# The total decay of ten late chunks taken from the last row of an exponential and spread over the partitions by two small DMAs

## The chip, the cores and the metric

The kernel runs on one core of one Trainium2 chip. The core has a TensorE for matmuls (PE in the profile, its weight loads PEld), a VectorE (DVE), a ScalarE (ACT), a GpSimd (POOL) and a SyncE (SP), whose instruction stream issues nearly all DMAs here. Each engine works through its own instructions strictly in order; an instruction that waits holds up everything behind it on that engine. SBUF is the on-chip memory with 128 partitions; PSUM is the memory that PE writes to, eight banks of 2 KB per partition. The metric is the device time of one execution in microseconds, the median of several runs.

## The reference, cut to what matters

```python
def _attn_ref(q, k, v, alpha):                 # 4 x 8 heads x 768 steps x 48
    for t in range(S):
        state = alpha[:, :, t, :, None] * state + np.einsum('bhd,bhe->bhde', k[:, :, t], v[:, :, t])
        y[:, :, t] = np.einsum('bhd,bhde->bhe', q[:, :, t], state)

def _moe_ref(x, w_in, w_spatial, b_spatial, w_out):
    h = np.maximum(x @ w_in, 0.0)              # 384 -> 1024
    u, v = h[..., :512], h[..., 512:]
    v_n = (v - mean(v)) / np.sqrt(var(v) + 1e-06)
    v_s = np.einsum('ts,bsd->btd', w_spatial, v_n) + b_spatial[None, :, None]
    return (u * v_s) @ w_out
```

The first half is a linear attention whose state (48 x 48 per head) decays by `alpha`, a factor for each step and each of the 48 rows. Its output, laid out as 4 x 768 x 384, goes through the second half, a gated MLP that also mixes over the 768 steps.

## The kernel before, in words

**Chunks.** Each of the 4 batches is cut into 6 chunks of 128 steps, so chunks have numbers 0 to 23, and chunk 6b is the first of batch b. Inside a chunk the recurrence is done by matmuls: with A the running product of `alpha` in the chunk, q is multiplied by A, k is divided by A, and the state that is handed on is (old state + k'v) times A at the chunk's last step. This last factor, one number for each head and row, is the *total decay*.

**Steps of one late chunk** (`single(i)`, used for chunks 10 to 23; the early ones are done two or four at a time by other functions). I name them as the code does:

- `acs`, `kcs`, `qcs`, `vcs` (L883): four loads of 192 KB from alpha, k, q, v, issued by SP.
- `lns` (ACT, L888): the logarithm of alpha. `cums` (PE): one matmul with a triangle of ones (L898) puts the running sums of the logarithms into a PSUM bank, with steps on the 128 partitions; four more matmuls with one column each (L901) put the *total* of each row into four spare columns of the same bank, this time with (head, row) on the partitions.
- `einvs` (ACT, L908) = exp(-sums) in SBUF, and `eexps` (ACT, L910) = exp(sums), written back over the sums in PSUM.
- `ebc` (ACT, L915): two small exponentials take the totals from the spare columns into the tile `bc`, (head, row) on the partitions. Chunk 11, 17 and 23 are the last of their batch and need no total.
- `kts`, `qts` (L189): k times `einvs` (mostly POOL), q times `eexps` (DVE). `trk` (PE, L988) turns both for a pair of chunks, `evs` (ACT, DVE) copies them out; `upd` (PE, L932) is k'v; `sc`, `ms`, `y`, `xe` make the chunk's output x.
- The carry: `z` (DVE, L393) = k'v + old state; `S` (L189, on DVE for the first chunk of a batch and for chunk 19, else on POOL) = z times `bc`; `sb`, a bf16 copy. `y` of the next chunk and `S` of the next chunk need it.

**The MLP** runs between the chunks, a batch behind: `v`, `u`, `s`, `o` are its matmuls (all recorded at L1005), `ve`, `ue`, `bn`, `rs`, `nm`, `vn`, `se`, `g`, `oe` the steps of DVE, ACT and POOL between them; `vn` is the normalised v, `s` the mixing over steps. `st` (L1184, SP) stores 192 KB of output.

**What sets the order.** A table, `PLAN`, lists every step with its engine and its PSUM banks. The kernel emits the steps in that order, so each engine's queue is fixed in advance, SP's included. A word such as `S549` is step 549 on SP. SP's queue in the stretch that the change touches reads: ... vcs 14, kcs 14, acs 17, qcs 17, kcs 16, vcs 15, qcs 16, kcs 17, vcs 16, then the loads of chunks 18 to 21 in a mixed order (the last of them vcs 20), a store, and the loads of chunks 22 and 23.

Of the kernel before, what the change touches and what calls it, by code (L numbers as in the profile page):

```python
# [15 lines left out]
FP32 = mybir.dt.float32  # L16
# [44 lines left out]
S548 S611 S561 S551 S549 A358 A363 D418 D423 P511@7 P369@3 P413@0 P374@2 P380@1 D414 D417 A261 A512 P378@0 D422 A498  # L61
D364 A375 A564 P263@5 P499@6 G244 G332 G409 G256 A370 A379 A513 D371 G415 A500 A501 P419@0 P424@3 A425 G517 G505 G503
D381 D382 D516 G515 A420 P266@2 P269@4 A502 A365 A383 A270 D366 D504 P429@0 P426@1 P438@3 P440@6 D384 A368 A430 A427
P436@4 A437 A441 A385 D264 D439 P272@0 D367 D267 D428 D431 D386 P521@1 P372@4 A514 A273 P565@6 P376@2 A377 A432 A552
P442@7 A568 P529@0 D443 D522 P456@3 D433 D434 A435 A566 A567 D373 P452@7 P553@1 P518@2,5 A519 A554 A556 D520 A555 P457
D458 D530 D570 G569 G523 G557 G459 P444@4 P445 P448@5 D446 P453 D454 P468@6 P449 D558 D450 P533@7,4 P524@2,0 P572@1,3
D525 G451 G455 P472@5 P469 P460@2 P473 D526 D534 D535 G531 G447 D474 S623 A559 P575@7 D576 A573 P461 S625 S612 S563
A615 D470 D462 P616@4 P527@5 P536@1 A627 S613 A574 P579@7,3 P588@6,0 G577 A617 A528 D589 A618 A537 P628@5 A629 A571
G475 P538@2 A630 P464@1 S624 S614 S730 S718 S721 S626 S720 G620 D621 D581 D580 S733 S732 P476@6 G631 G578 P541@3
P584@7 A539 A619 A542 P465 S784 S719 A477 D632 P634@5,4 D590 A636 D466 D585 S731 A722 P591@3 S786 S772 S785 S773 S835  # L70
S774 A592 S787 S775 G622 G532 P582@1 A583 D635 D540 P637@7 P482@6 A633 A483 P723@5 G586 G471 D638 G639 A724 P645@3,4
P640@0,2 D543 G463 G587 P479@7 P604@6 P596@1 D646 D642 D641 A734 A726 D647 G729 G467 A605 A741 G727 P593@3 P600@6 A594
P735@0 D606 D595 A738 D480 P648@4 P643@3 A544 D545 D546 D597 A649 P488@2 A644 A788 A601 A489 D547 P653@4 P660@7 P745@6
A654 D746 D655 A736 A607 D608 D610 P491@3 P664@4 A661 A665 A737 P650@6 A492 A776 G739 P598@1 D651 D609 P485@4 D652
A486 A725 D747 P666@7 A667 D740 P602@6 P662@4 P789@3 A656 A603 P676@7 P672@0 P753@6 A599 A790 A791 P777@1 A778 A792
A779 S484 S847 S836 S837 A839 A783 S838 S848 A663 S849 D657 D658 D659 D754 D728 P677 P673 P680@6 P688@5 D674 P681
P668@0 D794 D755 D678 D782 G781 G795 D682 P799@7 P669 G793 D800 P689 G675 D690 D670 P742@6,4 P796@7,3 A851 A780 D797
P696@5 A743 A798 G683 G679 P808@0 P697 P852@7 P840@6 A841 A842 A853 A843 A854 D744 P748@3,4 P757@1,2 D698 G801 G671
D749 D809 D758 P692@5 P693 D694 D750 P684@3 P703@0 P685 P700@5 G846 D759 A701 D686 P706@4 D856 D845 D707 A704 P760@5
A761 P751@0 A752 A802 P803@6,7 D805 G844 G855 P812@3,2 P858@4,5 G810 G687 G699 G691 A859 G695 D813 P762@0 S850 P861@7  # L80
P765@3 D814 D804 P712@2 P815@6 A756 A763 P806@0 A860 D862 D764 D857 A816 A807 A766 P864@5,7 P869@4,1 S702 P715@6 D866
D871 D767 D870 D865 P828@7 A829 D830 P824@1 P820@3 P817@7 A821 A768 A818 A825 G863 P872@4 A873 S705 A716 S481 S259
S268 S487 S265 S493 S490 S271 S708 S262 S478 S274 G811 P867@5 D819 P826@3 P822@1 D868 P877@4 D769 D771 A827 S717 A831
A823 A878 A770 A713 D832 P874@3 D833 D834 P890@5 P888@1 P884@4 D879 D875 D876 A880 D881 D882 P916@6 P709@2 A710 P896@3
P886@7 P900@0 A887 A889 A885 A891 P892@2 D883 P897 D898 G899 P893 P901 P908@5 P909 D894 D902 P904@2 P905 G903 P917
P912@0 P913 P920@3 D906 D895 D918 G919 D907 P929@6 P923@2 P921 S711 A930 S931 A924 S925 S714 D914 D910 D911 P926@6
G915 D922 P932@2 A933 D927 S928 S934 P938@3 D939 S940 P935@6 A936 S937 P941@3 D942 S943
"""
# [4 lines left out]
QUADS = (0,3)  # L93
PLAIN = (0, 2)
IDLE = 16

# [35 lines left out]
def kernel(  # L132
# [38 lines left out]
    def sb(name, n, shape, dt=BF16):  # L171
        return [consts.tile(shape, dt, name=f"{name}{x}") for x in range(n)]
# [189 lines left out]
    def half(x):  # L362
        return slice(64 * x, 64 * x + 64)
# [64 lines left out]
    def pair(j):  # L428
# [72 lines left out]
        def ebc(_):  # L501
            src = banks[sl_c[1].bank][:, DM:DM + 2 * HP].rearrange("p (hp c) -> p hp c", c=2)
            for s in range(2):
                nc.scalar.activation(out=bcs[j % 4][half(s), :, :, s], in_=src[half(s)], func=AF.Exp)

# [60 lines left out]
        for i in chunks:  # L566
            carry(i, sl_t[i], ("upd", j, "pair"), bcs[j % 4][:, :, i % 2])

# [301 lines left out]
    def single(i):  # L870
# [25 lines left out]
        def cum(_):  # L896
            cm = flat(sl_c)
            nc.tensor.matmul(out=cm[:, 0:DM], lhsT=le_one, rhs=la[:, :, :, 0:D], start=True, stop=True)  # L898
            if not last:
                for hp in range(HP):  # L900
                    nc.tensor.matmul(  # L901
                        out=cm[:, DM + hp:DM + hp + 1], lhsT=la[:, hp].rearrange("p s d -> p (s d)"), rhs=ones_col,
                        start=True, stop=True)

        op(("cums", i), "PE", cum, [("lns", i), ("one",), ("zeros", 2)], take=[sl_c],
           pe=(0.0, 384, 0, 2) if last else (0.241, 1, 0, 10))
        buf = binv[i % 4].rearrange("p (hp s) d -> p hp s d", s=2)
        op(("einvs", i), "ACT", lambda _: nc.scalar.activation(out=buf, in_=sums(), func=AF.Exp, scale=-1.0),  # L908
           [("cums", i)] + readers("kt", j - 2), use=[sl_c])
        op(("eexps", i), "ACT", lambda _: nc.scalar.activation(out=sums(), in_=sums(), func=AF.Exp), [("einvs", i)], use=[sl_c])  # L910
        bc = bcs[j % 4][:, :, ci]
        if not last:
            def ebc(_):
                for s in range(2):
                    nc.scalar.activation(out=bc[half(s), :, s], in_=banks[sl_c.bank][half(s), DM:DM + HP], func=AF.Exp)  # L915
# [312 lines left out]
    for th in range(2):  # L1228
        made[("bb", th)].deps.append(made[("cum", 1, 1)])
    idle = consts.tile([128, 1], FP32, name="idle")  # L1230
    nc.vector.memset(junk, 0.5)  # L1231
# [33 lines left out]
```

## Time and profile before

| what | value |
|---|---|
| time, median of 3 runs (lowest to highest) | 138.53 us (138.37 to 139.0) |
| span of the profiled execution, first to last instruction | 137.9 us |
| PE busy | 130.1 us, 94% |
| DVE / ACT / POOL busy | 120.2 (87%) / 107.7 (78%) / 86.6 us (63%) |
| granted PE clock | 1.00 throughout |
| the chain that ended last | PE 60%, DMA 19%, POOL 8% |

The profiled execution has no time of its own beside its span; the 0.6 us between its span and the median lie before its first and after its last instruction.

How to read the rows: in a timeline a row gives start and length in us, engine, source line, operation, output tile <- input tiles, form and count; instructions of the same kind are merged to one row with `xN`. What stands in brackets is the idle time before it and what ended it. `SPq` is SP's queue: the length of its row is the time that the issue of the DMA held the queue, waiting included. A group's row ends with busy time and mean length in ns, then the idle time before the group's instructions.

### The profile page before, as it was taken

The numbers are of one execution on the slowest core, as the hardware profiler recorded it, in microseconds if no ns is written. First come the engines' busy times: TensorE is split into PE (matmuls) and PEld (weight loads), VectorE is DVE, ScalarE is ACT, GpSimd is POOL, SyncE is SP. The second block draws the span as 40 slices with busy tenths as digits, with TensorE's granted clock in tenths as the row PEclk, the third lists the DMA queues.
The fourth block names the chain that finished last, engine by engine and source line by source line (L and its number), as shares of the span: only waits on it lengthen the run. The fifth ranks groups of instructions, "written<-read, shape, count | busy, mean of one in ns | idle before, by whom it ended". The sixth has DMA issues, their size and how long they took to land.

```text
span 137.9 us, 5298 instructions
## 1 busy us (share of the span) xinstructions
PE 130.1 (94%) x2108; PEld 79.4 (58%) x2122; DVE 120.2 (87%) x300; ACT 107.7 (78%) x261; POOL 86.6 (63%) x146
## 2 busy tenths in 40 slices
PE   6999998999999999799999999999999999999990
PEld 3365555565566556466657676656576765566560
DVE  6259999989989999899899999997999999974960
ACT  3476998999999799699997989999865796953040
POOL 7355899993499799761079989520799841004550
PEclk9999999999999999999999999999999999999999
DMA  3999999499989788699999898999960597101064
GB/s 88 370 372 381 344 349 361 106 373 382 355 162 281 159 168 165 124 186 188 193 204 201 164 209 156 189 186 216 213 134 5 187 349 270 63 0 57 0 233 172
DMA packets 76521, 28.66 MB, mean 208 GB/s; under 512 B 63056, under 2 KB 74960, under 8 KB 76496
## 3 DMA queue, kind: packets, MB, share of 16 engines
q1 hardware_dynamic: 76464, 28.32, 77.8%
q8 instruction: 16, 0.26, 0.8%
q14 instruction: 9, 0.07, 0.2%
q0 software_dynamic: 32, 0.00, 0.0%
HBM read 23.60 MB, written 4.72 MB: 205 GB/s over the span
## 4 chain that ended last, share of the span: by engine, by line
PE 60%; DMA 19%; POOL 8%; issue 3%; SPq 3%; ACT 3%; DVE 0%; POOLq 0%; ACTq 0%
PE bank L1005 43%; DMA raw_w<-in_moe_w_spatial_dram 6%; DMA kc<-in_k_dram 5%; DMA raw_w<-in_moe_w_out_dram 4%; DMA ac<-in_alpha_dram 4%; PE bank L960 3%; SPq L883 3%; PE bank L944 2%; PE bank L988 2%; PE bank L416 2%; POOL w_row L180 2%; POOL kt L189 2%; PE bank L932 1%; PE bank L898 1%; POOL state L189 1%
## 5 line engine op out<-in xcount | busy, mean ns | idle before, releaser
L1005 PE MATMUL bank<-w_spT,vn 128*128 128x384 bf16 x192 | 35.6, 327 | 0.0
L189 POOL TENSOR_TENSOR gT<-vs,uT 128x384 bf16<-128x384 f32 x28 | 25.7, 933 | 14.1 <-DVE vs L1152 14.1
L189 POOL TENSOR_TENSOR kt<-kc,binv 128x384 bf16<-128x384 f32 x22 | 20.2, 928 | 22.3 <-ACT binv L908 15.2
L1005 PEld LDWEIGHTS <-vn 128*128 128x128 bf16 x192 | 17.5, 98 | 11.2 <-issue 0.3
L1005 PE MATMUL bank<-w_in,xT 128*128 128x512 bf16 x58 | 17.4, 380 | 1.6 <-ACT xT L178 0.7
L1005 PE MATMUL bank<-xT,w_in 128*128 128x384 bf16 x96 | 18.7, 326 | 0.0
L1005 PE MATMUL bank<-w_out_sb,gT 128*128 128x384 bf16 (+1 forms) x100 | 18.4, 320 | 0.0
L1152 DVE TENSOR_TENSOR vs<-bank,bsp_bc 128x384 f32<-128x384 f32 x31 | 16.3, 549 | 2.4 <-PE bank L1005 2.3
L949 DVE TENSOR_TENSOR ptm<-bank,mask 128x512 bf16<-128x512 f32 x28 | 17.9, 682 | 0.5 <-PE bank L944 0.3
L178 ACT COPY kqT<-bank 128x512 bf16<-128x512 bf16 (+1 forms) x20 | 15.0, 793 | 3.1 <-PE bank L988 1.9
L1067 DVE BATCH_NORM_STATS2 stats<-v_sb 128x6 f32<-128x512 bf16 x24 | 16.4, 683 | 0.6 <-ACT v_sb L184 0.5
L184 ACT ACTIVATE v_sb<-bank 128x512 bf16<-128x512 f32 x20 | 11.7, 597 | 2.0 <-PE bank L1005 1.7
L184 ACT ACTIVATE uT<-bank 128x384 bf16<-128x384 f32 x27 | 12.4, 494 | 0.7 <-PE bank L1005 0.6
L1005 PEld LDWEIGHTS <-w_in 128*128 128x128 bf16 x96 | 9.0, 97 | 6.7 <-DVE ptm L949 0.3
L189 DVE TENSOR_TENSOR qt<-qc,bank 128x384 bf16<-128x384 f32 x24 | 12.6, 545 | 0.2 <-DMA qc<-in_q_dram 0.2
L1005 PEld LDWEIGHTS <-gT 128*128 128x128 bf16 x100 | 9.2, 98 | 5.8
L178 ACT CAST xT<-bank 128x384 bf16<-128x384 f32 x23 | 10.4, 482 | 1.1 <-PE bank L416 0.8
L843 DVE TENSOR_TENSOR ptm<-bank,mask 128x512 bf16<-128x512 f32 x16 | 10.3, 683 | 0.2 <-PE bank L836 0.2
L242 PE MATMUL bank<-junk 128*128 128x512 f32 (+3 forms) x14 | 8.8, 763 | 1.0 <-DVE junk L1231 1.0
L1005 PEld LDWEIGHTS <-xT 128*128 128x128 bf16 x72 | 6.2, 97 | 6.2 <-ACT xT L178 1.2
L178 ACT COPY raw_w<-bank 128x384 f32<-128x384 f32 x8 | 3.8, 479 | 7.3 <-PE bank L1005 7.2
L393 DVE TENSOR_TENSOR zs<-bank,state 128x384 f32<-128x384 f32 x16 | 8.8, 548 | 0.5 <-PE bank L932 0.4
(162 smaller groups left out, 264.3 us busy)
## 6 DMA issues: line engine op xcount, KB each, us to landing
ac<-in_alpha_dram SPq DMA_DIRECT2D x14, 192.0 KB, 4.4
kc<-in_k_dram SPq DMA_DIRECT2D x14, 192.0 KB, 4.4
qc<-in_q_dram SPq DMA_DIRECT2D x14, 192.0 KB, 4.4
vc<-in_v_dram SPq DMA_DIRECT2D x14, 192.0 KB, 4.2
raw_w<-in_moe_w_spatial_dram SPq DMA_DIRECT2D x3, 768.0 KB, 7.8
out_dram<-raw_w SPq DMA_DIRECT2D x11, 192.0 KB, 2.1
out_dram<-o_sb SPq DMA_DIRECT2D x9, 192.0 KB, 2.0
ac<-in_alpha_dram SPq DMA_DIRECT2D x2, 768.0 KB, 6.7
```

The source lines that it names most:

```text
L178: nc.scalar.copy(out=out, in_=in_)
L184: nc.scalar.activation(out=out, in_=in_, func=AF.Relu)
L189: ENG[eng].tensor_tensor(out=out, in0=in0, in1=in1, op=ALU.mult)
L242: nc.tensor.matmul(out=banks[n][:, 0:cols].rearrange("p (a b) -> p a b", a=4), lhsT=junk, rhs=junk[:, None, 0:cols // 4].to_broadcast([128 ...
L393: lambda _: nc.vector.tensor_tensor(out=zs[i % 3], in0=tp(), in1=state[(i - 1) % 3], op=ALU.add),
L843: nc.vector.tensor_tensor(out=ptm[n2][:, ci, s], in0=banks[sl.bank].rearrange("p (hp t) -> p hp t", hp=HP), in1=mask[:, 3][:, None, :].to_ ...
L883: nc.sync.dma_start(out=t[x].rearrange("p hp s d -> p (hp s) d"), in_=src[b, :, c * C:c * C + C, :].rearrange("h s d -> s h d"))
L949: nc.vector.tensor_tensor(out=ptm[n2][:, ci, s], in0=banks[sl_p[s].bank].rearrange("p (hp t) -> p hp t", hp=HP), in1=mask[:, 2][:, None, : ...
L960: nc.tensor.matmul(out=place(to, 3 * hp + (0, 1, 1, 2)[x]), lhsT=heads(vb, hp, x), rhs=ptm[n2][:, ci, x // 2, hp, :], start=(turn == 0), s ...
L1005: nc.tensor.matmul(out=ps, lhsT=lhsT, rhs=rhs, start=first and n == 0, stop=last and n == len(pairs) - 1)
L1067: nc.vector.bn_stats(out=stats[tt % 2], in_=v_sb[n2][:, tt, :])
L1152: nc.vector.tensor_tensor(out=vs[d], in0=banks[sl.bank][:, 0:TH], in1=bsp_bc[:, th, :], op=ALU.add)
```

## The change

For the ten chunks of the list `BY_DMA` (12 to 22 without 17) the total decay is no longer computed on its own. `cums` loses its four one-column matmuls, and the two `ebc` exponentials on ACT are gone. Instead `eexps` writes exp(sums) to SBUF in fp32 (into one of three tiles of `o_sb`, which are used in turn, with the elements arranged so that one partition's row is ordered by half, row and head pair). The last of its 128 partitions, step 127, holds the total decay, and two DMAs on SP's queue (one for each half, 48 partitions x 4 fp32 values) spread it over the partitions of `bc`. `qts` reads exp(sums) from this SBUF tile instead of the PSUM bank. The layout of `bc` is turned so that the four values of a partition lie together.

`PLAN` gets ten `ebc` words on SP and loses ten on ACT; `eexps` of chunk 18 moves ahead on ACT, to just behind `einvs` 18. All other words stay in their order on their engines. In SP's queue the new words come to stand as follows: `ebc` 13, 12, 15 and 14 between kcs 14 and acs 17; `ebc` 16 between qcs 16 and kcs 17; `ebc` 18, 19, 21 and 20 between vcs 20 and the store; `ebc` 22 between qcs 23 and vcs 23. Because the three tiles are used in turn, `eexps` of a chunk also waits for `qts` and the two DMAs of the chunk three places earlier in the list.

```diff
-D364 A375 A564 P263@5 P499@6 G244 G332 G409 G256 A370 A379 A513 D371 G415 A500 A501 P419@0 P424@3 A425 G517 G505 G503
+D364 A375 A564 P263@5 P499@6 G244 G332 G409 G256 A370 A379 A513 S514 D371 G415 A500 A501 S502 P419@0 P424@3 A425 G517
...
+BY_DMA = (13, 12, 15, 14, 16, 18, 19, 21, 20, 22)
...
-    bcs = sb("bc", 4, [128, HP, 2, 2], FP32)
+    bcs = sb("bc", 4, [128, 2, 2, HP], FP32)
...
-            if not last:
+            if not last and i not in BY_DMA:
                 for hp in range(HP):
                     nc.tensor.matmul(
                         out=cm[:, DM + hp:DM + hp + 1], lhsT=la[:, hp].rearrange("p s d -> p (s d)"), rhs=ones_col,
                         start=True, stop=True)
...
-        op(("eexps", i), "ACT", lambda _: nc.scalar.activation(out=sums(), in_=sums(), func=AF.Exp), [("einvs", i)], use=[sl_c])
-        bc = bcs[j % 4][:, :, ci]
-        if not last:
+        bc = bcs[j % 4][:, ci].rearrange("p s hp -> p hp s")
+        if i in BY_DMA:
+            before = BY_DMA.index(i) - 3
+            decay = o_sb[1 + (before + 2) % 3].rearrange("p (s d hp) -> p s d hp", hp=HP, s=2)
+            made[("decay", i)] = op(
+                ("eexps", i), "ACT", lambda _: nc.scalar.activation(out=decay.rearrange("p s d hp -> p hp s d"), in_=sums(), func=AF.Exp),
+                [("cums", i)] + ([(x, BY_DMA[before]) for x in ("qts", "ebc")] if before >= 0 else [
...
+            def ebc(_):
+                for s in range(2):
+                    nc.sync.dma_start(
+                        out=bcs[j % 4][64 * s:64 * s + D, ci, s], in_=decay[C - 1:C, s])
+
+            op(("ebc", i), "SP", ebc, [("eexps", i), ("zeros", 0), ("S", i - 8)])
...
-        op(("qts", i), "DVE", lambda e: mul(e, qt[:, :, :, 0:D], t["qc"], sums()),
-           [("eexps", i), ("qcs", i), ("zeros", 1 + n2)] + old_q(j), use=[sl_c])
+        op(("qts", i), "DVE", lambda e: mul(e, qt[:, :, :, 0:D], t["qc"], decay.rearrange("p s d hp -> p hp s d") if i in BY_DMA else sums()),
+           [("eexps", i), ("qcs", i), ("zeros", 1 + n2)] + old_q(j), use=[] if i in BY_DMA else [sl_c])
```

More of the change, by code (lines that the diff above doesn't have):

```diff
@@ L69 @@
[L69 to L87, printed above, removed]
+A615 D470 D462 P616@4 P527@5 P536@1 A627 S613 A574 P579@7,3 P588@6,0 G577 A617 A528 D589 A618 S619 A537 P628@5 A629
@@ L503, in ebc @@
             for s in range(2):
-                nc.scalar.activation(out=bcs[j % 4][half(s), :, :, s], in_=src[half(s)], func=AF.Exp)
+                nc.scalar.activation(out=bcs[j % 4][half(s), :, s].rearrange("p c hp -> p hp c"), in_=src[half(s)], func=AF.Exp)
         op(("ebc", j, "pair"), "ACT", ebc,
@@ L566, in pair @@
         for i in chunks:
-            carry(i, sl_t[i], ("upd", j, "pair"), bcs[j % 4][:, :, i % 2])
+            carry(i, sl_t[i], ("upd", j, "pair"), bcs[j % 4][:, i % 2].rearrange("p s hp -> p hp s"))
         for par in range(2):
@@ L905, in single @@
         op(("cums", i), "PE", cum, [("lns", i), ("one",), ("zeros", 2)], take=[sl_c],
-           pe=(0.0, 384, 0, 2) if last else (0.241, 1, 0, 10))
+           pe=(0.0, 384, 0, 2) if last or i in BY_DMA else (0.241, 1, 0, 10))
         buf = binv[i % 4].rearrange("p (hp s) d -> p hp s d", s=2)
@@ L909, in single @@
            [("cums", i)] + readers("kt", j - 2), use=[sl_c])
-        op(("eexps", i), "ACT", lambda _: nc.scalar.activation(out=sums(), in_=sums(), func=AF.Exp), [("einvs", i)], use=[sl_c])
-        bc = bcs[j % 4][:, :, ci]
-        if not last:
+        bc = bcs[j % 4][:, ci].rearrange("p s hp -> p hp s")
[5 more added lines that the diff above has]
+                [("cums", i)] + ([(x, BY_DMA[before]) for x in ("qts", "ebc")] if before >= 0 else [
+                    x for jj in QUADS for x in [("pm", 2 * jj + y) for y in range(4)] + [("upd", jj, "pair"), ("upd", jj + 1, "pair")]]),
+                use=[sl_c])
+            def ebc(_):
[3 more added lines that the diff above has]
+            op(("ebc", i), "SP", ebc, [("eexps", i), ("zeros", 0), ("S", i - 8)])
+        else:
+            op(("eexps", i), "ACT", lambda _: nc.scalar.activation(out=sums(), in_=sums(), func=AF.Exp),
+               [("einvs", i)], use=[sl_c])
+        if not last and i not in BY_DMA:
             def ebc(_):
@@ L1229 @@
         made[("bb", th)].deps.append(made[("cum", 1, 1)])
+    for n in range(12, 15):
+        made[("oe", n)].deps += [made[x, i] for x in ("qts", "ebc") for i in BY_DMA[(n - 11) % 3::3]]
     idle = consts.tile([128, 1], FP32, name="idle")
```

26 lines of the change are left out of this document (22 added, 4 removed).

## The prediction

> **What bounds the kernel now.** I read the page first: shares, slices, DMA issues.
>
> ```profile
> PE 130.1 (94%) x2108; PEld 79.4 (58%) x2122; DVE 120.2 (87%) x300; ACT 107.7 (78%) x261; POOL 86.6 (63%) x146
> ...
> PE   6999998999999999799999999999999999999990
> ...
> DMA  3999999499989788699999898999960597101064
> ...
> PE 60%; DMA 19%; POOL 8%; issue 3%; SPq 3%; ACT 3%; DVE 0%; POOLq 0%; ACTq 0%
> ...
> kc<-in_k_dram SPq DMA_DIRECT2D x14, 192.0 KB, 4.4
> ...
> out_dram<-o_sb SPq DMA_DIRECT2D x9, 192.0 KB, 2.0
> ```
>
> PE is full from slice 17 on (58 us), so any later PE wait adds to the time. DMA is nearly full as well until slice 29. A late load lands 4.4 us after its issue, a store into an emptier queue after 2.0. Next the windows, for the stretch of the new DMAs.
>
> ```profile
> 66.00:96.00 30.00, 29.83 (x469) 19.26 (x470) 28.62 (x67) 27.50 (x71) 18.38 (x24) 1.00 0.96 191
> ```
>
> The columns are window, length, busy PE, PEld, DVE, ACT, POOL, clock, DMA share, GB/s. PE has 0.17 us free in 30, DVE 1.4, and the DMA share is 0.96: loads that fall behind cannot be caught up. Then SP's timeline, since the change puts twenty DMAs and their waits into that queue.
>
> ```profile
> 65.16 0.73 SPq L883 DMA_DIRECT2D kc<-in_k_dram  x1
> 65.99 1.43 SPq L883 DMA_DIRECT2D ac<-in_alpha_dram  x1
> ...
> 71.19 0.79 SPq L883 DMA_DIRECT2D kc<-in_k_dram  x1
> ...
> 80.96 0.37 SPq L883 DMA_DIRECT2D ac<-in_alpha_dram  x1
> ...
> 90.53 2.14 SPq L883 DMA_DIRECT2D vc<-in_v_dram  x2
> 92.75 0.66 SPq L1184 DMA_DIRECT2D out_dram<-w_row  x1
> 93.46 0.42 SPq L883 DMA_DIRECT2D ac<-in_alpha_dram  x1
> ```
>
> These are, in order: kcs 14, acs 17, kcs 17, acs 21, then vcs 21 with vcs 20, a store, acs 23. SP issues without a break. Its queue runs far behind the written order: vcs 20 leaves only at 92.67.
>
> **The change part by part.** First the consumers of the total decay on DVE, in the chunks that begin a batch, and ACT's steps.
>
> ```profile
> 67.11 0.55 DVE L189 TENSOR_TENSOR state<-bank,bc 128x384 f32<-128x384 f32 x1
> 67.57 0.32 DVE L1084 TENSOR_SCALAR shift<-mvs,rstd 128x1 f32<-128x1 f32 x2
> ...
> 90.33 0.56 DVE L189 TENSOR_TENSOR state<-bank,bc 128x384 f32<-128x384 f32 x1
> ...
> 92.16 0.68 DVE L186 TENSOR_SCALAR v_sb<-bank 128x512 bf16<-128x512 f32 x1
> ```
> ```profile
> 67.99 0.81 ACT L1092 ACTIVATE vn<-v_sb,shift,rstd 128x512 bf16<-128x512 bf16 x1 [0.20 <-DVE shift L1084]
> 68.83 0.49 ACT L908 ACTIVATE binv<-bank 128x384 bf16<-128x384 f32 x1
> 69.22 0.49 ACT L910 ACTIVATE bank<-bank 128x384 f32<-128x384 f32 x1
> ...
> 70.91 0.35 ACT L915 ACTIVATE bc<-bank 64x4 f32<-64x4 f32 x2
> 71.28 0.47 ACT L910 ACTIVATE bank<-bank 128x384 f32<-128x384 f32 x1
> ...
> 76.87 0.50 ACT L910 ACTIVATE bank<-bank 128x384 f32<-128x384 f32 x1
> ...
> 85.01 0.35 ACT L915 ACTIVATE bc<-bank 64x4 f32<-64x4 f32 x2
> ...
> 97.39 0.47 ACT L910 ACTIVATE bank<-bank 128x384 f32<-128x384 f32 x1
> ```
> ```profile
> 67.89 0.33 PE L898 MATMUL bank<-la,le_one 128*128 128x384 bf16 x1
> 68.05 0.24 PE L901 MATMUL bank<-ones_col,la 128*128 128x1 bf16 x4
> 68.23 0.41 PE L988 MATMUL bank<-ident,kt 64*128 64x64 bf16 x16
> ...
> 68.80 0.50 PE L1005 MATMUL bank<-w_spT,vn 128*128 128x384 bf16 x2
> ...
> 93.00 1.63 PE L1005 MATMUL bank<-xT,w_in 128*128 128x384 bf16 x9
> ```
>
> The DVE rows at 67.11 and 90.33 are `S` 12 and `S` 18; L910 at 69.22, 71.28, 76.87 and 97.39 is `eexps` 15, 14, 16 and 20; the ACT pair at 85.01 is `ebc` 18, in time for `S` 18 by 5 us.
>
> Removed on PE: ten times four one-column matmuls. From 68.05 to the next start they take 0.18 us, so at most 1.8 in all; I take 0.15 each. Seven of the ten lie ahead of `S` 18 and vanish in the wait there (below); chunks 21, 20 and 22 keep 3 x 0.15 = 0.5 us.
>
> Removed on ACT: ten pairs at 0.35 us, 3.5 us. ACT is 3% of the chain; I count nothing, except that `eexps` 14 comes 0.35 earlier. `eexps` into SBUF: bounds 0.47 and 0.50 from its own rows, as the output's size is the same; nothing. The bank that is now free before `qts` has no waiter; nothing. `eexps` 18 moves ahead of one logarithm, which comes 0.5 us later; its load was early and PE has the matmul after it much later, nothing. The turned `bc` feeds the same multiplications with the same count; nothing, and at most the 0.1 between the readers' own rows.
>
> Added, wait 1, `S` 12. No row shows these small DMAs. The issue costs between 0.37 (shortest load) and the 0.73 to 1.43 of the rows above; I take 0.4, since there is little to describe. `ebc` 13 and 12 are four issues from 65.99, the last done at 67.6. They land no sooner than 67.6 + 2.0 = 69.6 and no later than 67.6 + 4.4 = 72.0. I take 69.6, which is also when kcs 14 ahead of them lands (65.16 + 4.4). `S` 12 thus starts 2.5 us late. Queued behind it on DVE is the shift for `vn` (67.57); ACT waits for that shift already now (row 67.99), and PE's row at 68.80 reads this `vn`. So DVE, ACT and PE are all about 2.5 late.
>
> Added, wait 2, SP. `ebc` 15 waits for `eexps` 15, `ebc` 14 for `eexps` 14, and acs 17 stands behind both. `eexps` 14 ends at 71.28 + 0.47 + 2.5 - 0.35 = 73.9; with two issues acs 17 leaves at 74.7 instead of 65.99. The DMA queue has run empty, which the row of 0.96 says cannot be made good. Five loads follow at about 0.65 each, until 78.0. Then `ebc` 16 waits for `eexps` 16, 76.87 + 0.50 + 2.5 = 79.9, and kcs 17 leaves at 80.7 instead of 71.19. It lands after 2.4 us (a store's 2.0, and a little for its smaller pieces), at 83.1 instead of 71.19 + 4.4 = 75.6: the loads are 7.5 us late from here on.
>
> Added, wait 3, `S` 18, the one that decides. `ebc` 18 stands behind vcs 20. That load's issue held the queue to 92.67; starting at about 91.9, the middle of the row of two, it lands at 96.3, with the 7.5 at 103.8, its issue ending about 100.2. Two issues make 101.0, plus 2.0 is 103.0; if the small ones must pass behind the load, 103.9. I take 103.0. `S` 18 stood at 90.33: 12.7 us late. DVE waits, and with it everything behind: `ve` (92.16 to 92.84) frees the bank that PE's row at 93.00 fills, 0.2 us of slack. PE stands still by 12.5 us against before, and waits 1 and 2 are contained in this, not added.
>
> [...]
>
> Added, wait 4: `ebc` 20 holds acs 23 (93.46) until `eexps` 20 (97.39 + 0.47) and the store are through, about 5.5 us beyond its place on the shifted clock. Its logarithm and those of ACT's copies behind it come late; between nothing and 1.2 us reach PE, I take 0.3, since PE has other work queued there.
>
> The new waits for the reuse of the three tiles (`eexps` 14 on `ebc` 13, `eexps` 20 on `qts` and `ebc` 18) end before the ones above: `ebc` 13 lands ahead of `ebc` 12, and `eexps` 20 stands 7 us behind `S` 18, which waits for the same DMA. Nothing; were `ebc` 13 slower, its delay would enter wait 2 one for one.
>
> `qts` on DVE now reads two SBUF tiles. Rows by shape:
>
> ```profile
> L189 DVE TENSOR_TENSOR qt<-qc,bank 128x384 bf16<-128x384 f32 x24 | 12.6, 545 | 0.2 <-DMA qc<-in_q_dram 0.2
> ...
> L189 DVE TENSOR_TENSOR gT<-vs,uT 128x384 bf16<-128x384 f32 x3 | 2.2, 730 | 0.0
> ```
>
> Between 0 and 185 ns more for each, 1.9 us for ten. In the main case DVE has idle time from its waits, and I count nothing; uncovered it costs those 1.9.
>
> Sum: 12.5 - 0.5 + 0.3 = 12.3 us. The profiled execution spans 137.9, the median is 138.53, so I add to the median: **150.8 us**.
>
> **The rivals.**
> *Faster.* The ten small DMAs land before their readers, and what is left is the removed work: 138.5 less 1.1 (between 0.5 and 1.8) is 137.4. The place that decides is `S` 18: SP would have to issue `ebc` 18 by 88. The row at 90.53 speaks against it: the two loads ahead are not out before 92.67. Chance 0.05.
> *No change.* As that, but `qts` loses its PSUM operand and pays 1.9: 139.3, or about 138.5 where half of them meet POOL at work. [...] Chance 0.02.
> *The place alone.* The queue does not fall behind in wait 2, because the loads in flight are enough; `ebc` 18 then leaves at 93.5 and lands at 95.5 to 97.1, `S` 18 is 5.2 to 6.8 late: about 144. For it: a load has some us to spare before its user. Against it: DMA's 0.96. Chance 0.15.
> *Worse.* The small DMAs cost 0.8 to issue and 4.4 to land. `S` 12 then waits until 65.99 + 3.2 + 4.4 = 73.6, 4 us more than I took, and the queue falls that much further behind: about 155. Chance 0.15.
>
> **How the numbers follow.** The main case has 0.63; its own range is 148 to 154, by the two landings and the issue price. From 144 to 156 all but the two good cases and the outer halves of the other two are held, some 0.2 outside. Faster or slower means by more than 0.5%, 0.7 us, about what a measurement of this kernel can tell from no change. Faster 0.05, same 0.02, slower 0.93.
>
> **What would show it.** In the profile after: `S` of chunks 12 and 18 on DVE with idle time ended by the DMA into `bc`, about 2 and 7 us or more; SPq rows on the new line with long waits ahead of acs 17 and acs 23, and DMA slices that drop there; PE digits below 9 near 69 and 95 to 103; no L901 row for the ten chunks; `qt` on DVE between 545 and 730 ns. I am wrong if `S` 18 does not wait, if SP gets past `eexps` 14 without a pause, or if PE finds other work while DVE stands.

## The result, and the profile after

The changed kernel takes 162.31 us (median of six runs, 160.96 to 163.99) against 138.36 us of the kernel before on the same chip (138.09 to 139.0): a ratio of 1.169, 95% interval 1.166 to 1.173. It is slower by 24.0 us, where 12.3 were forecast; the time lies outside the range of 144 to 156. The sign and the mechanism that was to decide came as forecast, the size did not. Ratios and intervals, here and below, leave out the executions that the chip ran in a slower state, while the medians keep them, so a ratio can lie a little below the quotient of its medians.

The page of the kernel after, with the rows that were shown of before: shares, slices of 4 us, the chain that ended last.

```profile
PE 136.3 (85%) x2082; PEld 78.7 (49%) x2082; DVE 126.3 (79%) x300; ACT 107.8 (67%) x241; POOL 89.5 (56%) x146
...
PE   7999999999999999968885879009977889999991
...
PEclk9999999999999999999999999755999999999999
DMA  4999995999899899700759899750019569611036
...
PE 30%; DMA 23%; POOL 12%; ACT 11%; DVE 8%; SPq 8%; issue 6%; DVEq 0%; POOLq 0%; ACTq 0%
```

PE was full from slice 17 on (counted from 0); now thirteen of the slices 17 to 38 are below 9, and 25 and 26 (100 to 108 us) are empty. DMA drops to 0 at 68 to 76 and at 108 to 116 us (and once near the end, as before). The clock row has something new: in slices 25 to 27 it is at 0.7, 0.5 and 0.5, and in the last of these, 108 to 112 us, PE works again. The chain, three fifths PE before, is spread over DMA, POOL, ACT, DVE and the queue.

The waits of all engines, then those of SP's queue (waited-for, us in total, times, longest):

```profile
DVE state L190 <- DMA bc<-o_sb: 10.3, 2, 8.5
...
PE bank L1023 <- DVE state L190: 7.8, 1, 7.8
...
ACT la L889 <- DMA ac<-in_alpha_dram: 4.8, 3, 3.8
```
```profile
SPq L923 <- ACT o_sb L916: 12.4, 2, 8.3
```

L190 `state` is `S`, L923 the small DMAs, L916 `eexps` into SBUF. `S` 12 and `S` 18 wait 10.3 us together for small DMAs, PE once 7.8 us for `S` 18, and SP's queue 12.4 us for `eexps`. SP's timeline shows what stands behind:

```profile
64.87 0.95 SPq L884 DMA_DIRECT2D kc<-in_k_dram  x1
65.91 9.83 SPq L923 DMA_DIRECT2D bc<-o_sb  x8
75.78 0.59 SPq L884 DMA_DIRECT2D ac<-in_alpha_dram  x1
...
81.70 1.14 SPq L923 DMA_DIRECT2D bc<-o_sb  x2
83.33 0.38 SPq L884 DMA_DIRECT2D kc<-in_k_dram  x1
...
101.97 1.98 SPq L884 DMA_DIRECT2D vc<-in_v_dram  x2
104.04 2.28 SPq L923 DMA_DIRECT2D bc<-o_sb  x3
...
115.30 3.21 SPq L923 DMA_DIRECT2D bc<-o_sb  x4
118.57 0.57 SPq L1202 DMA_DIRECT2D out_dram<-w_row  x1
119.19 0.43 SPq L884 DMA_DIRECT2D ac<-in_alpha_dram  x1
```

acs 17 leaves at 75.78 instead of 65.99, kcs 17 at 83.33 instead of 71.19, `ebc` 18 at 104.04 behind vcs 20, acs 23 at 119.19 instead of 93.46. On DVE and PE this gives:

```profile
69.69 0.56 DVE L190 TENSOR_TENSOR state<-bank,bc 128x384 f32<-128x384 f32 x1 [1.82 <-DMA bc<-o_sb]
...
107.16 0.56 DVE L190 TENSOR_TENSOR state<-bank,bc 128x384 f32<-128x384 f32 x1 [8.48 <-DMA bc<-o_sb]
```
```profile
107.77 1.44 PE L1023 MATMUL bank<-w_in,xT 128*128 128x512 bf16 x3 [7.80 <-DVE state L190]
```

`S` 12 is 2.6 us later than before, `S` 18 16.8. The page's groups (busy, mean ns, idle before) show the changed instructions:

```profile
L190 DVE TENSOR_TENSOR qt<-qc,o_sb 128x384 bf16<-128x384 f32 x10 | 10.9, 1091 | 1.8 <-DMA qc<-in_q_dram 1.8
```
```profile
L916 ACT ACTIVATE o_sb<-bank 128x384 f32<-128x384 f32 x10 | 8.8, 884 | 0.8 <-DVE qt L190 0.8
```

For `qts`, 545 ns became 1091. The second row, of all groups, is `eexps`: 884 ns in place of 470 to 500.

### The profile page after: what moved, and what is told of

Its sections match the earlier page's. It is cut to its first block, busy times and chain, and to the rows that moved or that the text cites. A ratio compares the mean times of both kernels' runs of the same rounds, so it can differ in the third digit from the quotient of the medians.

```text
span 160.2 us, 5249 instructions
## 1 busy us (share of the span) xinstructions
PE 136.3 (85%) x2082; PEld 78.7 (49%) x2082; DVE 126.3 (79%) x300; ACT 107.8 (67%) x241; POOL 89.5 (56%) x146
## 4 chain that ended last, share of the span: by engine, by line
PE 30%; DMA 23%; POOL 12%; ACT 11%; DVE 8%; SPq 8%; issue 6%; DVEq 0%; POOLq 0%; ACTq 0%
PE bank L1023 23%; SPq L884 6%; DMA raw_w<-in_moe_w_spatial_dram 5%; DMA raw_w<-in_moe_w_out_dram 4%; DMA kc<-in_k_dram 4%; DMA vc<-in_v_dram 3%; POOL gT L190 3%; ACT kqT L179 3%; DMA bc<-o_sb 2%; DMA qc<-in_q_dram 2%; POOL kt L190 2%; DVE qt L190 2%; DMA ac<-in_alpha_dram 2%; ACT o_sb L916 2%; SPq L923 2%
## 5 line engine op out<-in xcount | busy, mean ns | idle before, releaser
L190 POOL TENSOR_TENSOR kt<-kc,binv 128x384 bf16<-128x384 f32 x22 | 20.8, 953 | 40.0 <-ACT binv L909 27.8
L1023 PE MATMUL bank<-w_spT,vn 128*128 128x384 bf16 x192 | 36.1, 326 | 0.2
L190 POOL TENSOR_TENSOR gT<-vs,uT 128x384 bf16<-128x384 f32 x28 | 26.9, 977 | 14.7 <-DVE vs L1170 14.7
L1023 PE MATMUL bank<-w_in,xT 128*128 128x512 bf16 x72 | 19.8, 389 | 11.2 <-DVE state L190 7.8
L1023 PEld LDWEIGHTS <-vn 128*128 128x128 bf16 x192 | 17.6, 98 | 12.3 <-issue 1.0
L1023 PE MATMUL bank<-xT,w_in 128*128 128x384 bf16 x96 | 19.8, 339 | 0.0
L1023 PE MATMUL bank<-w_out_sb,gT 128*128 128x384 bf16 (+1 forms) x100 | 19.3, 328 | 0.5 <-ACT v_sb L185 0.2
L1023 PEld LDWEIGHTS <-w_in 128*128 128x128 bf16 x96 | 9.5, 102 | 7.9 <-issue 1.9
L185 ACT ACTIVATE uT<-bank 128x384 bf16<-128x384 f32 x27 | 12.4, 494 | 1.1 <-PE bank L1023 1.0
L190 DVE TENSOR_TENSOR qt<-qc,o_sb 128x384 bf16<-128x384 f32 x10 | 10.9, 1091 | 1.8 <-DMA qc<-in_q_dram 1.8
L179 ACT CAST xT<-bank 128x384 bf16<-128x384 f32 x23 | 10.6, 490 | 2.2 <-PE bank L417 1.4
L889 ACT ACTIVATE la<-ac 128x384 bf16<-128x384 f32 x14 | 7.2, 539 | 4.8 <-DMA ac<-in_alpha_dram 4.8
```

What stands on the lines that cost most here:

```text
L179: nc.scalar.copy(out=out, in_=in_)
L185: nc.scalar.activation(out=out, in_=in_, func=AF.Relu)
L190: ENG[eng].tensor_tensor(out=out, in0=in0, in1=in1, op=ALU.mult)
L889: op(("lns", i), "ACT", lambda _: nc.scalar.activation(out=la[:, :, :, 0:D], in_=t["ac"], func=AF.Ln), [("acs", i), ("zeros", 2 * n2)] + [ ...
L1023: nc.tensor.matmul(out=ps, lhsT=lhsT, rhs=rhs, start=first and n == 0, stop=last and n == len(pairs) - 1)
```

## The experiments

Medians are given beside the kernel before on the same chip (138.2 to 138.7 us each time). SP's words are written as in the text above, `ebc` standing for a pair of small DMAs; where a diff shows only a queue's order, the other engines' orders are those of the kernel after.

**place: the small DMAs early.** Only SP's order differs: each pair stands where its values are there in time.

```diff
-qcs14 acs14
+qcs14 ebc13 ebc12 acs14
...
-kcs14 ebc13 ebc12 ebc15 ebc14 acs17
+kcs14 acs17
...
-vcs15 qcs16 ebc16 kcs17 vcs16
+vcs15 ebc15 qcs16 kcs17 ebc14 vcs16
...
-vcs17 qcs18
+vcs17 ebc16 qcs18
...
-qcs21 acs20
+qcs21 ebc18 acs20
...
-vcs20 ebc18 ebc19 ebc21 ebc20 st8 acs23
+vcs20 st8 ebc19 acs23
...
-vcs22 kcs23 qcs23 ebc22 vcs23
+vcs22 ebc21 kcs23 ebc20 qcs23 vcs23 ebc22
```

> The changed kernel, every instruction kept, only SP's queue reordered: each pair of small DMAs stands where SP arrived, in the kernel before, at about the time its exponential was done (ebc 12 and 13 behind qcs 14, ebc 15 behind vcs 15, ebc 14 behind kcs 17, ebc 16 behind vcs 17, ebc 18 behind qcs 21, ebc 19 behind the store, ebc 21 behind vcs 22, ebc 20 behind kcs 23, ebc 22 last). Theory Q (the place in SP's queue is the cost: readers wait for DMAs that leave late, loads wait behind exponentials): S 12 and S 18 wait for nothing, PE's clock stays at 1.00, and only the dearer qts (1.09 us for 0.55) and eexps (0.88 for 0.49) are left, 139 to 144 us. Theory L (the layout with 16-byte steps and the SBUF operand cost most, on DVE and ACT): 152 us or more, with the shift growing evenly over the ten chunks.

Measured: 144.11 us, ratio 1.043 (1.036 to 1.049). `S` 18 no longer waits for its DMA; the timelines of SP and DVE:

```profile
86.54 0.76 SPq L884 DMA_DIRECT2D qc<-in_q_dram  x1
87.43 1.21 SPq L923 DMA_DIRECT2D bc<-o_sb  x2
```
```profile
92.36 0.56 DVE L190 TENSOR_TENSOR state<-bank,bc 128x384 f32<-128x384 f32 x1 [0.38 <-ACT v_sb L185]
```

162.3 - 144.1 = 18.2 of the 24.0 us are the places in SP's order. But 5.8 us remain although only one state still waits for its pair (1.3 us, on GpSimd), and my sum did not have them.

**strided and natural: the forms without DMAs.** In both, the totals and their exponentials stand as before and no small DMA is issued; `eexps` writes to SBUF and `qts` reads there. strided keeps the change's arrangement, where neighbouring elements of a head pair lie 16 bytes apart; natural writes them side by side.

```diff
-            decay = o_sb[1 + (before + 2) % 3].rearrange("p (s d hp) -> p s d hp", hp=HP, s=2)
+            decay = o_sb[1 + (before + 2) % 3].rearrange("p (hp s d) -> p hp s d", hp=HP, s=2)
```

> No small DMAs: total decays by the four one-column matmuls and the two small ACT exponentials as before, in their old places; but eexps of the ten chunks writes to the SBUF tile in the order half, row, head pair, and qts reads it there, as in the change. Theory Q: 10 x 0.55 us more on DVE and 10 x 0.39 on ACT, DVE being busy 28.6 of 30 us: 140 to 144 us. Theory L: 150 us or more.

> As strided, but the SBUF tile has the elements in the order in which q has them, so that nothing is written or read in steps of 16 bytes. If the steps make eexps and qts dear, they are back at 0.49 and 0.55 us and the time is 138 to 139.5. If the second SBUF operand makes qts dear, qts stays near 1.1 us, eexps goes back to 0.49, and the time is within 1 us of strided.

Measured: strided 143.83 us (1.039, 1.035 to 1.043), natural 140.33 us (1.014, 1.011 to 1.018), which lies between its two expectations. Groups of strided, then of natural:

```profile
L190 DVE TENSOR_TENSOR qt<-qc,o_sb 128x384 bf16<-128x384 f32 x10 | 11.4, 1137 | 0.1
L916 ACT ACTIVATE o_sb<-bank 128x384 f32<-128x384 f32 x10 | 8.9, 885 | 0.5 <-DVE qt L190 0.5
```
```profile
L190 DVE TENSOR_TENSOR qt<-qc,o_sb 128x384 bf16<-128x384 f32 x10 | 8.0, 799 | 0.0
...
L916 ACT ACTIVATE o_sb<-bank 128x384 f32<-128x384 f32 x10 | 5.0, 498 | 0.2 <-DVE qt L190 0.2
```

With the operand in SBUF `qts` takes 250 ns more on average, and the kernel 2.0 us. The average hides two cases, as natural's timeline of DVE and POOL shows:

```profile
70.57 0.91 POOL L190 TENSOR_TENSOR gT<-vs,uT 128x384 bf16<-128x384 f32 x1
70.63 1.26 DVE L190 TENSOR_TENSOR qt<-qc,o_sb 128x384 bf16<-128x384 f32 x1
...
93.49 0.55 DVE L190 TENSOR_TENSOR qt<-qc,o_sb 128x384 bf16<-128x384 f32 x1
```

Three of the ten `qts` began while GpSimd ran nothing; they took 540 to 553 ns, as from PSUM (546 on average). The other seven began during a GpSimd instruction, took 700 to 1259 ns, and each ended 0.41 to 0.42 us after that instruction's end. So it is not the operand that costs, but the meeting with GpSimd. The steps of 16 bytes cost `eexps` 390 ns more and `qts` 340 (300 where GpSimd ran nothing: 841 and 845 ns in strided), and the kernel 3.5 us. Together the forms cost 5.5 us, counted at nothing in the prediction.

**unread: the places without the waits of `S`.** SP's order is that of the change, but the DMAs write a tile that nobody reads; totals as before.

```diff
-                        out=bcs[j % 4][64 * s:64 * s + D, ci, s], in_=decay[C - 1:C, s])
+                        out=spares[j % 4][64 * s:64 * s + D, ci, s], in_=decay[C - 1:C, s])
```

> The changed kernel with all small DMAs in their places in SP's queue, but they write a tile that nobody reads; the total decays come from the one-column matmuls and the ACT exponentials as before. So S waits for no DMA, while the loads still wait behind the small DMAs. If S 18's wait decides, as I put it (12.5 of my 12.3 us), most of the gain comes back: 146 to 151 us, with the loads' lateness and the layout left. If the loads behind the exponentials decide alone, the time stays at 157 to 163.

Measured: 150.42 us (148.78 to 152.9; 1.083, 1.076 to 1.090). Against strided that is 6.6 us more by the medians and 6.1 by the ratios, for loads that leave late behind DMAs which wait for `eexps`. The other 162.3 - 150.4 = 11.9 us of the change need the waits for the DMAs, those of `S` above all (`eexps` waits for no DMA here either).

**late18: one pair late.** place, with `ebc` 18 alone behind vcs 20.

```diff
-qcs21 ebc18 acs20
+qcs21 acs20
...
-vcs20 st8
+vcs20 ebc18 st8
```

> The kernel with the small DMAs in timely places (run place), except the pair for chunk 18, which goes back behind vcs 20 as in the change. In place it landed at 90.5 and S 18 ran at 92.4; behind vcs 20 it lands with or just after that load, 97.8. Theory Q: S 18 about 5.6 us later, and all of it on PE, so 149 to 151 us against 144.1; if PE's idle stretch also lowers its granted clock, up to 2 us more. If S 18's wait is covered: within 1 us of place.

Measured: 150.69 us (1.087, 1.083 to 1.092), 6.6 above place. DVE's and SP's timelines:

```profile
92.73 1.76 SPq L884 DMA_DIRECT2D vc<-in_v_dram  x2
94.58 1.69 SPq L923 DMA_DIRECT2D bc<-o_sb  x2
```
```profile
97.77 0.56 DVE L190 TENSOR_TENSOR state<-bank,bc 128x384 f32<-128x384 f32 x1 [6.21 <-DMA bc<-o_sb]
```

`S` 18 starts 97.77 - 92.36 = 5.4 us later and the time rises by 6.6; the granted clock, 1.00 in place, averages 0.977 here, which can be the other 1.2. This is the prediction's rival "the place alone", measured: the wait that decides needs no late loads.

**seconds: all but chunks 12 and 18.** The change, with these two chunks left as before.

```diff
+OLD = (12, 18)
+        spread = [x for x in BY_DMA if x not in OLD]
```

> The changed kernel with its places in SP's queue, but chunks 12 and 18, whose S stands on DVE as the first of a batch, keep the old way: totals by matmul, ebc on ACT, eexps in PSUM; eight chunks stay with DMAs. S 12 and S 18 wait for no DMA; the loads still wait behind ebc 15, 14, 16, 19, 21 and 20. Theory Q: S 18's wait was worth 8.5 of idle DVE and the clock behind it, so 146 to 151 us, like unread. If the loads' lateness decides alone: 157 us or more.

Measured: 147.36 us (1.067, 1.061 to 1.072). Eight pairs in the change's places cost 3.3 us beyond place; the pairs of 12 and 18, whose states stand on DVE ahead of PE's next work, the other 162.3 - 147.4 = 14.9. As these two chunks also have the old forms in seconds, about 1 us (two tenths of 5.5) of the 14.9 belongs to the forms, and the eight pairs cost that much more than 3.3.

**warm: PE kept busy during its wait.** The change, with nine additions of idle matmuls of 512 columns ahead of the matmul that waits.

```diff
-P650@6
+P650@6:512#1:512#1:512#1:512#1:512#1:512#1:512#1:512#1:512#1
```

> The changed kernel with nine matmuls on constants (0.76 us each, into a PSUM bank that nobody uses then) ahead of the matmul that waits for S 18, so that PE works through most of the 7.8 us in which it stood. Nothing else differs. If PE's idle stretch is what lowered its granted clock (0.50 and 0.64 in 102 to 114 us), the clock stays at 1.00 there, the 4.4 us from that matmul to the next waiting one shrink to about 2.3, and the time is 159 to 161 us. If the clock fell for another reason, 162 us or slightly more.

Measured: 159.72 us (157.68 to 159.89; 1.150, 1.144 to 1.156), 2.6 less than the change although PE does more. The windows of the kernel after, then of warm (length, busy PE, PEld, DVE, ACT, POOL, clock, DMA share, GB/s):

```profile
102.00:108.00 6.00, 0.23 (x1) 0.10 (x1) 0.84 (x2) 0.01 (x1) 0.00 (x0) 0.50 0.73 139
108.00:114.00 6.00, 6.00 (x24) 2.88 (x23) 4.44 (x15) 2.00 (x6) 0.00 (x0) 0.64 0.00 0
```
```profile
101.00:107.00 6.00, 6.00 (x21) 2.71 (x21) 2.90 (x9) 0.00 (x0) 0.00 (x0) 1.00 0.26 48
107.00:113.00 6.00, 6.00 (x42) 3.60 (x40) 5.39 (x12) 5.08 (x12) 2.06 (x2) 1.00 0.01 0
```

PE's timeline of the kernel after, behind the row at 107.77 shown above, then of warm at the same work:

```profile
113.23 0.33 PE L899 MATMUL bank<-la,le_one 128*128 128x384 bf16 x1
```
```profile
105.13 0.81 PE L1024 MATMUL bank<-w_in,xT 128*128 128x512 bf16 x3
...
108.38 0.33 PE L900 MATMUL bank<-la,le_one 128*128 128x384 bf16 x1
```

With PE idle the clock was 0.50 and 0.64, with PE kept busy 1.00. The stretch from the waiting matmul to the next `cums` takes 113.23 - 107.77 = 5.5 us in the kernel after, 108.38 - 105.13 = 3.3 in warm: 2.2 us, near the 2.6 of the medians. The profiled execution of warm is its fastest one, whose `S` 18 comes earlier by itself, so the medians are what counts. Neither figure is exact: the idle matmuls lasted 1.0 us longer than the wait in the profiled execution, and in the other three the mean clock was 0.978 to 0.989, so there the gap was not wholly filled (0.968 in the profiled execution of the kernel after).

**row: `qts` back in PSUM.** place's SP order; `eexps` stays in the bank, and a further exponential of the last 32 partitions, just ahead of it on ACT, fills the SBUF tile that the DMAs read.

```diff
+                nc.scalar.activation(
+                    out=decay[96:128], in_=sums()[96:128].rearrange("p hp s d -> p s d hp"), func=AF.Exp)
+                nc.scalar.activation(out=sums(), in_=sums(), func=AF.Exp)
```

> Timely places in SP's queue, and the exponential of the sums stays in PSUM, where qts reads it as before; one more ACT exponential takes the last 32 partitions from PSUM into the SBUF tile for the small DMAs, writing without steps and reading PSUM in steps. So qts is back at 0.55 us, eexps at 0.49, ACT has 0.5 us for the 0.35 of the old pair, PE is rid of the one-column matmuls (1.1 to 1.8 us in all). If the rest of the change is free when layout and place are right: 136.8 to 138 us. If the twenty DMAs in the loads' queue cost by themselves: 138.5 to 140.

Measured: 142.84 us (1.031, 1.027 to 1.034), above both expectations. `qts` is back at 544 ns, but the addition stands in the way of `eexps`:

```profile
L190 DVE TENSOR_TENSOR qt<-qc,bank 128x384 bf16<-128x384 f32 x24 | 12.6, 544 | 1.0 <-ACT bank L918 0.8 <-DMA qc<-in_q_dram 0.2
L916 ACT ACTIVATE o_sb<-bank 32x384 f32<-32x384 f32 x10 | 4.8, 483 | 0.2
```

It takes 483 ns for 32 partitions, as long as the one for 128 (475 on average in this run), where the pair it replaces took 0.35 us later in ACT's order. That the strided side is here the read, from PSUM, and that it costs nothing, shows that the 390 ns above belong to the strided write. `qts` waits only 0.8 us for `eexps`; most of the 4 us must be elsewhere, and inert, below, shows where they can come from.

**copyrow and inert: are small DMAs in good places free?** copyrow is the kernel before with every order kept: at the place of the pair on ACT stands one instruction that takes the last 32 rows to SBUF, PE makes no total, and DMAs in timely places spread the row. inert is the kernel before with nothing removed, and twenty small DMAs from a constant tile into a tile that nobody reads in the same places.

```diff
+    for n, i in enumerate((12, 13, 15, 14, 16, 18, 19, 21, 20, 22)):
+        def spread(_, i=i):
+            for s in range(2):
+                nc.sync.dma_start(
+                    out=spares[i // 2 % 4][64 * s:64 * s + D, i % 2, s],
+                    in_=mask.bitcast(FP32)[127:128].rearrange("p a b -> p (a b)")[:, 0:D * HP])
+        op(("spread", i), "SP", spread, [("zeros", 0)])
```

> The kernel before, every engine's order kept; for the ten chunks TensorE makes no total, and the pair of exponentials on ScalarE is replaced, at the same place in its order, by one that takes the last 32 rows of the sums (an exp, or a copy where the second exponential has been there already) into a tile in SBUF, from which two small DMAs in timely places spread the last row; the second exponential stays in PSUM and the product reads it there. If places and forms are the whole loss (my theory), this stays near the time before: TensorE has up to 0.5 us less to do on its path, ScalarE 0.483 (measured in row) in place of 0.35 for the pair, so 0 to 1.3 more where nothing hides it: 137.5 to 139.5 us. If the transfers themselves cost something (rival), S waits for them even in their places, and it comes to 140 us or more, like row's 142.8.

> The kernel before with nothing taken away and twenty small DMAs of the change's form added to the loads' queue in the same timely places, from a constant tile into a tile that nobody reads. My theory: an issue of some 0.58 us and a landing right behind the load ahead cost nothing where the loads have slack: 138.2 to 139.2 us. Rival: they push the loads behind them, each pair by 1.2 us, and the time rises by 1.2 us or more: 139.5 to 142 us. If inert is near before and place is not, the 0.3 us between strided and place is no price of the transfers.

Measured: copyrow 144.2 us (1.034, 1.028 to 1.040); inert 142.25 us (140.65 to 143.29; 1.019, 1.013 to 1.026). My theory falls: DMAs that do nothing and are waited for by nothing cost 2.7 us by the ratio and 3.5 by the medians. SP's timeline of inert, then its waits on POOL:

```profile
82.51 1.44 SPq L1235 DMA_DIRECT2D sp<-mask  x2
...
84.67 0.53 SPq L885 DMA_DIRECT2D ac<-in_alpha_dram  x1
...
98.30 0.43 SPq L885 DMA_DIRECT2D ac<-in_alpha_dram  x1
```
```profile
POOL kt L190 <- DMA kc<-in_k_dram: 7.5, 3, 4.3
```

acs 21 leaves at 84.67 instead of 80.96, acs 23 at 98.30 instead of 93.46. SP issues without a break in this stretch, and a pair holds it 1.44 us here. POOL then waits 7.5 us for loads of k, where in the kernel before it was

```profile
POOL kt L189 <- DMA kc<-in_k_dram: 0.5, 1, 0.5
```

copyrow adds waits of its states to that, in its view of waits:

```profile
POOL state L191 <- DMA bc<-o_sb: 2.5, 1, 2.5
POOL sbd L191 <- DMA bc<-o_sb: 1.9, 1, 1.9
DVE state L191 <- DMA bc<-o_sb: 1.6, 1, 1.6
```

**inert_pool: the same from POOL.** GpSimd issues the DMAs of inert, at places where it stood idle.

```diff
-                nc.sync.dma_start(
+                nc.gpsimd.dma_start(
-        op(("spread", i), "SP", spread, [("zeros", 0)])
+        op(("spread", i), "POOL", spread, [("zeros", 0)])
```

> As inert (142.25 us, 3.5 above before), but GpSimd issues the twenty small DMAs, in places where it stood idle in the kernel before, and SyncE's order is that of before. In inert SyncE issued back to back from 57 to 107 us, and loads left up to 7.9 us later. If the issue on SyncE is the price (theory I), the loads leave as before and this stays at 138.2 to 139.5 us, the upper end if an issue on GpSimd holds up a product or a state there. If the transfers themselves are the price, because their pieces hold up the loads on the DMA engines (theory T), it is at 141 to 143 us as in inert.

Measured: 142.18 us (141.58 to 143.17; 1.029, 1.024 to 1.033), no better. The loads leave earlier than in inert now, and POOL waits less for them. Its waits, the new tile's view and the page's chain:

```profile
POOL kt L190 <- DMA kc<-in_k_dram: 2.7, 1, 2.7
```
```profile
L1235 POOL DMA_DIRECT2D sp<-mask x20: 502/503/567, 61.2 to 109.2; - x20
```
```profile
PE 53%; POOL 23%; ACT 8%; DMA 4%; issue 4%; DVE 4%; SPq 0%; POOLq 0%; DVEq 0%; ACTq 0%
```

But each issue now stands 0.50 us on POOL, a pair 1.06 with its gaps, and POOL is 23% of the chain, where before it was 8%. `kts` 20 still starts 0.4 us earlier than in the profile of before; the products `g` of batch 2 behind the pairs of 21 and 20 start 0.6 and 1.7 us later. The time is the one that theory T named, 141 to 143 us, but T's mechanism, transfers that hold up the loads, is not seen: the loads issued between 55 and 105 us take 4.1 us to land at the median, as in the kernel before, and unread_timely, below, has the same number of transfers at no cost. I read it so that the price of issuing went with the issue, from one queue that had no room to another; that is argued from these rows and not tested by itself.

copyrow with its DMAs issued by GpSimd has no measured time, so that combination is open.

**unread_timely: the same DMAs where the products are late.** unread's kernel with place's order on SP.

> The kernel of strided (143.83 us), with twenty small DMAs in the timely places of place, from the second exponential's tile into a tile that nobody reads; totals and their exponentials stand as before. place (144.11 us) is this kernel without the totals on TensorE and ScalarE, and with the states waiting for the DMAs. Theory A: the prices of the parts add, so that the DMAs cost here what they cost in inert (3.5 us): 146.5 to 148 us, and leaving the totals out is worth some 3 us in place. Theory H: with products 5 us late the loads have that much more slack, and the issue time on SyncE is hidden here, where in inert it was not: 143.8 to 145 us, and leaving the totals out is worth 0 to 0.9 us, as predicted (0.5).

Measured: 143.72 us (1.038, 1.034 to 1.042), as strided without any DMA (143.83). Twenty such issues, which cost inert some 3 us, cost nothing that can be told here: with the products on ACT and DVE slower, the loads have room for them. (Their places are place's, which are not quite inert's.) And place, which leaves the totals out, is no faster (144.11): theory H, the prices do not add.

**What the 24.0 us are made of.** 5.5 the slower forms (strided against before); 0 the DMAs in timely places beside them (unread_timely), and about 0.4, within the intervals, for place against it; 18.2 the change's places in SP's order. Of these, 6 to 7 are late loads (unread against unread_timely) and the other 11 to 12 the waits for the DMAs, those of `S` above all, of which 2 to 3 come through the clock (warm). The split within the 18.2 is by differences between kernels; since prices do not add here, it is a reading and no exact account.

## Why the prediction was wrong, step by step

Two terms of the sum failed. The forms were taken at nothing and cost 5.5 us by themselves. And the waits that decide were mis-sized: `S` 18 came 16.8 us late instead of 12.7, and what follows it, taken at -0.2, cost another 5.8.

*Removed on PE, 0.5 us gained.* Nothing is seen: place is not faster than unread_timely, which keeps the totals. As one state in place waits 1.3 us for its pair, a gain of this size could be hidden.

*Wait 1, `S` 12.* Right: 2.59 us late where 2.5 were predicted; the pair for chunk 12 landed at 69.57 (69.6 predicted), 0.84 us behind kcs 14 ahead of it. The closeness is partly luck: the last of the four issues was done at 68.42, not 67.6, and landed 1.15 us behind that, not 2.0; two errors that cancel.

*Wait 2, SP.* Right in kind, too small. acs 17 left at 75.78 (74.7 predicted), kcs 17 at 83.33 (80.7), and landed at 86.18 (83.1): 10.6 us behind the 75.6 that the prediction took for before, not 7.5, and 11.2 behind the 75.00 that before's trace has. Of the 2.6 us by which kcs 17 left later than predicted, 1.8 are `eexps` 16, which let its first small DMA start at 81.70 and not 79.9, and 0.8 the issues. The issue price of 0.4 us was wrong, as the view of the tile `bc` shows:

```profile
L923 SPq DMA_DIRECT2D bc<-o_sb x20: 501/582/1011, 65.9 to 126.5; - x20
...
DMA to landing us min/median/max: 1.6/1.8/3.0
```

No issue took under 0.5; the lower bound, 0.37, was the shortest load. The longer `eexps` (884 ns) stands twice in this path.

*Wait 3, `S` 18, the one that decides.* The place and the mechanism were right: it waited for `ebc` 18 behind vcs 20. The term was mis-sized: 12.7 predicted, 16.8 measured. vcs 20's issue ended at 103.95 instead of 100.2, from wait 2, and `ebc` 18 landed at 107.04 instead of 103.0. The two small ones landed right behind the load ahead of them: vcs 20 at 106.73, they at 106.88 and 107.04 (the first one 2.8 us after its issue began, against 1.7 for the first one of `ebc` 21, which had no load ahead); in place they landed 0.16 and 0.33 us behind qcs 21, in late18 0.20 and 0.41 behind vcs 20. With a landing behind vcs 20, the 103.9 of the prediction, the sum would have been 0.9 higher, which is not what was missing. PE's waiter was another: not the bank that `ve` frees, but the one that `S` 18 itself reads, as PE's row at 107.77 names.

*Behind `S` 18.* Here 0.5 off and 0.3 on were predicted, as if PE then ran as before. From `S` 18 to the end DVE fell another 5.8 us behind (16.8 to 22.6, by the two profiled executions). 2.2 are the lower clock after PE's wait. Then `ebc` 21 and 20 hold the queue until 118.5, so that ACT waits 3.8 us for acs 23 (wait 4, taken at 0.3; the row of 4.8 above), and `qts` 19 to 22 are slower.

*The forms.* This step failed outright. "bounds 0.47 and 0.50 from its own rows, as the output's size is the same; nothing" measured 884 ns: the size was the same, the step between elements was not, and no row of before showed a strided write. With elements 16 bytes apart the exponential takes 885 ns, side by side 498 (strided against natural); a price is measured for this step alone, as no run has another one. "Between 0 and 185 ns more for each" measured 546 more in the kernel after. The cover I named, DVE's idle time from its waits, did not hide this: place, where those waits are gone from DVE, still has the 5.8 us. The bound of 185 came from the mean of three contiguous rows, 730 ns; in before's trace they are 548, 548 and 1093, the last one begun during a GpSimd instruction and ended 0.42 us after it. natural, which is that case, has 250 on average. The prediction priced the second SBUF operand by that mean, and the 138.5 of its rival "no change", where half of the ten meet POOL at work, is its estimate without a row of such a meeting. natural has both cases one by one: 540 to 553 ns where GpSimd ran nothing at the start and 700 to 1259 ns where it did.

*The base.* Adding to the median was right, but the 0.6 us between span and median set an execution's span against another's time. In a run where both are known the kernel before has a span of 136.9 at 138.73 us, and the kernel after 160.2 at 162.31: 1.8 and 2.1 us lie around the span. By this the profiled execution of before, with its span of 137.9, ran about 1.3 us longer than the median, so the two profiles differ by 22.3 us where the medians differ by 24.0.

*The rivals.* "The place alone" is what late18 shows, +6.6 for a wait of 6.2. "Worse" named the right direction, late queue and dear issues, but 155 was still too near. "Faster" and "no change" needed timely places; with those it is 144.1, since the forms remain. With the forms mended (copyrow, 144.2) the small DMAs do not pay either.

What stays open: how much of the 11 to 12 us of the states' waits belongs to `S` 12, to `S` 18 and to those on POOL, which was not separated in the company of the late loads; and whether a queue with free room exists for the twenty issues, as neither SP nor POOL had it. No version tried beats the kernel before.

## What to carry to other kernels

A small DMA was priced here by its place in a queue, not by its bytes: it cost an issue of 0.5 to 0.6 us on a queue that may have no room, it landed behind the load ahead (0.15 to 0.41 us behind it for `ebc` 18), and whatever stood behind it waited for its producer (8.3 us at the longest). When an output's arrangement is turned to suit a DMA, price the engines that write and read the tile in that arrangement first; here they cost 5.5 us against a saving that could not be measured. And a price found by itself may vanish beside another one (unread_timely against inert), so measure parts in the company in which they run. Look at the single rows of a group before taking its mean for a bound: 730 ns stood for 548 and 1093.

## What the hardware showed that was not expected

- An ACT exponential of 128x384 fp32 that writes SBUF in steps of 16 bytes takes 885 ns, contiguous 498; reading PSUM in that order and writing contiguously 483 (at 32 partitions). A DVE product that reads one fp32 operand in those steps takes 1137 ns on average, contiguous 799, from PSUM 546; where GpSimd ran nothing at its start, 841 to 845 in steps and 540 to 553 contiguous.
- A DVE product with both inputs in SBUF that began during a GpSimd instruction ended 0.41 to 0.42 us after that instruction (seven of seven in natural); begun while GpSimd ran nothing (three of ten) it took 540 to 553 ns, as from PSUM (546).
- In 7.8 us without work PE's granted clock fell to 0.50, was 0.64 on average over the next 6 us, and that cost 2.2 to 2.6 us; in the profiled execution with idle matmuls in the gap it stayed at 1.00. In the kernel after, PE's last matmul before the wait ended at 99.97, and the clock was still 1.00 in the windows 100:101 and 101:102, 0.53 in 102:103 and 0.50 in 103:104 and 104:108. The prediction had a wait of 12.5 us and no term for it.
- In the kernel after, the issue of a DMA of 768 bytes held SP for 0.58 us (median, least 0.50), that of a load of 192 KB for 0.79 to 1.04 (medians of the four kinds, least 0.38). On POOL, in inert_pool, a DMA of 768 bytes took 0.50.
